# Loading w, k and r in runs of steps and turning them on VectorE in squares of 32, in a tuned attention-and-MLP kernel

One core of one Trainium2 chip. The metric is the device time of one execution in microseconds (us), the median of the runs of one kernel. All numbers from profiles are from one profiled execution of the kernel named.

## The reference

Attention by a recurrence with a decay, then a layer norm and a two-layer MLP with a residual. All in float32.

```python
batch, n_heads, seq, head_dim = (4, 8, 768, 48)

def _attn_ref(r, k, v, w, u):
    state = zeros((B, H, D, D)); y = zeros_like(r)
    for t in range(S):
        kt, vt, rt, wt = k[:, :, t], v[:, :, t], r[:, :, t], w[:, :, t]
        cur = einsum('bhd,bhe->bhde', u[None] * kt, vt)
        y[:, :, t] = einsum('bhd,bhde->bhe', rt, state + cur)
        state = wt[:, :, :, None] * state + einsum('bhd,bhe->bhde', kt, vt)
    return y

def _moe_ref(x, g_ln, w_ch1, w_ch2):            # x: (4, 768, 384)
    mu = mean(x); var = mean((x - mu) ** 2)
    xn = (x - mu) / sqrt(var + 1e-06) * g_ln
    return x + maximum(xn @ w_ch1, 0.0) @ w_ch2  # 384 -> 1536 -> 384
```

## The kernel before

The work is cut into eight **rounds** (four batches, two halves of 384 steps each). A round has two **units** of four heads, a unit two **pairs** of heads. Each round goes through six **levels**: in each, PE multiplies k by r for growing blocks of steps (`a_ps`), and VectorE multiplies r and k by the decay of the block (`grow`) and keeps the new part of the block matrix (`keep`). PE is TensorE, DVE VectorE, ACT ScalarE, POOL GpSimd; SP is the engine whose queue (SPq) issues 255 of the 260 transfers that the profile of before lists, PSUM the memory that PE's products are put in here (the tiles named `_ps`). The MLP of the round before is cut into small steps that are put between the levels, so that PE never runs dry. Each level has a list of **tasks** that is spread over its MLP steps: loads, turns, norms. In the timelines below each engine works through its instructions in program order: in the changed kernel POOL has the products for an own sum ready at 143.1 us, but DVE sums them at 162.23, behind eight squares that stand ahead of the sum, six of which wait for their loads.

The products need r, k and w with the head's dimension across partitions, the arrays have it along the row. So each tile is loaded with 128 steps across partitions, 192 bytes a row, and turned by PE. One **turn** below is one pair of one tensor of one unit: three matmuls and a copy (cuts are marked with `...`):

```python
def load(q, which="wkr", eng=SP):
    for nm in which:
        for c in range(TT):                       # TT = 3 tiles of 128 steps
            eng.dma_start(out=nat[nm][q % 2][:, c, :, 0:D], in_=steps(src_of(nm), q, c))

def turned(q, nm, pr):                            # one pair of one tensor of one unit
    ...
    ps = ps_t.tile([P, RN], F32, tag="t", ...)    # PSUM, two buffers
    for c in range(TT):
        PE.transpose(ps[:, ts(c, P)], nat[nm][q % 2][:, c, ts(pr, 2)]..., ident)
    ACT.copy(out=a[nm][:, ts(pr, RN)], in_=ps)

def own_products(q, eng):                         # POOL reads k and r as loaded
    rk = st[q]["ruk"] = p1.tile([P, TT, NH, D], F32, tag="rk", ...)   # p1: ONE buffer
    eng.tensor_tensor(out=rk, in0=nat["k"]..., in1=nat["r"]..., op=ALU.mult)
    ...
def own_sums(q):
    DVE.tensor_reduce(out=o, in_=st[q]["ruk"], axis=AX.X, op=ALU.add)
```

The tasks that matter, in the loop over rounds and levels:

```python
first = 3 if rnd == 2 else 1
if rnd > 1 and new and first <= lev < first + 3:
    m = lev - first                               # w, then k and r of one unit, then of the other
    tasks += each(turned, new[m - 1 : m], "kr", pairs) if m else each(turned, new, "w", pairs)
...
if lev == 3 and rnd > 1:
    ...
    if rnd > 2:
        moments(rnd - 1)
        tasks += each(norm, [rnd - 1])            # xn of the round before, on DVE
if lev == 4 and rnd > 2:
    tasks += each(turned_x, [rnd - 1], range(KC)) # PE turns xn for the MLP
    tasks += each(own_products, new[:1], [POOL])
...
if lev == NLEV - 1:                               # level 5
    ...
    if rnd > 2 and new:
        own_sums(new[0])
    if rnd == 2:
        tasks += each(own_products, new[:1], [POOL]) + each(own_sums, new[:1])
    ...
    tasks += each(own_products, new[1:], [POOL])  # needs the rk buffer back
    tasks += each(own_sums, new[1:]) + ...
```

So the turns for round `rnd + 1` stand in levels 1 to 3 of round `rnd`; only in round 2, for round 3, they stand in levels 3 to 5.

Of the kernel before, what the change touches and what calls it, by code (L numbers as in the profile page):

```python
# [9 lines left out]
F32 = mybir.dt.float32  # L10
# [42 lines left out]
def kernel(  # L53
# [13 lines left out]
    PE, ACT, DVE, POOL, SPO = (  # L67
        InOrder(tc, e) for e in (nc.tensor, nc.scalar, nc.vector, nc.gpsimd, nc.sync)
    )
    SP = nc.sync  # L70

    B, H, S, D = r.shape
    P = 128
    HP = 64
    C = 64
    NH = 4
    NP = NH // 2
    U = H // NH
    TT = 3
    RN = TT * P  # L80
# [3 lines left out]
    W = NK * P  # L84
# [6 lines left out]
    pairs = range(NP)  # L91
# [3 lines left out]
    p1 = ctx.enter_context(tc.tile_pool(name="p1", bufs=1))  # L95
    p2 = ctx.enter_context(tc.tile_pool(name="p2", bufs=2))
    p3 = ctx.enter_context(tc.tile_pool(name="p3", bufs=3))
    p4 = ctx.enter_context(tc.tile_pool(name="p4", bufs=4))
# [8 lines left out]
    units = [(b, f, g) for b, f in rounds for g in range(U)]  # L107
    NU = len(units)
# [24 lines left out]
    def load_rows(nm, q, eng):  # L133

        b, f, g = units[q]
        src = {"w": w, "k": k, "r": r}[nm]
        eng.dma_start(
            out=flat(nm, q)[:, 0 : NH * TT * D].rearrange("p (h x) -> p h x", h=NH),
            in_=src[b, ts(g, NH), ds(f * RN, RN)].rearrange("h (p c) d -> p h (c d)", c=TT),
        )  # L140

    def load_v(q, eng=SP):
        vn[q] = p4.tile([P, TT, NH, D], F32, tag="v", name=f"v{q}")
# [21 lines left out]
    for j in range(2):  # L165
        ACT.dma_start(
            out=sel[ds(HP * j, D), :, j], in_=u.rearrange("(r j) d -> j d r", j=2)[j]
# [23 lines left out]
    for lev in range(NLEV - 1):  # L191
        n = 1 << lev
        m = const.tile([P, C // n, n], I8, name=f"mask2_{lev}")
# [109 lines left out]

    st, carry = {}, {}

    def turned(q, nm, pr):
        a = st.setdefault(q, {})
        if pr == 0:
            if nm == "w":
                if q % U == 0:  # L310
                    st["w"] = p1.tile([P, U, W], F32, tag="w", name=f"wT{q // U}")
                a["w"] = st["w"][:, q % U]
            elif "rk" not in a:

                rk = a["rk"] = p4.tile([P, 2, W], F32, tag="rkT", name=f"rkT{q}")
                a["r"], a["k"] = rk[:, 0], rk[:, 1]
        ps = ps_t.tile([P, RN], F32, tag="t", name=f"{nm}_ps{q}_{pr}")
        if q < U:


            for c in range(TT):
                for j in (1, 0):
                    at = ((2 * pr + j) * TT + c) * D - HP * j
                    PE.transpose(
                        ps[0 : HP * (j + 1), ts(c, P)],
                        flat(nm, q)[:, ds(at, HP * (j + 1))], ident,
                    )
            (DVE.tensor_copy if q == 0 and pr else ACT.copy)(
                out=a[nm][:, ts(pr, RN)].rearrange("p (m c) -> p m c", c=TT),
                in_=ps.rearrange("p (c m) -> p m c", c=TT),  # L330
            )
            return
        for c in range(TT):
            PE.transpose(
                ps[:, ts(c, P)],
                nat[nm][q % 2][:, c, ts(pr, 2)].rearrange("p j d -> p (j d)"), ident,
            )
        ACT.copy(out=a[nm][:, ts(pr, RN)], in_=ps)
# [371 lines left out]
    def each(f, *ranges):  # L710
        calls = [()]
        for r_ in ranges:
            calls = [c + (x,) for c in calls for x in r_]
        return [lambda c=c: f(*c) for c in calls]
# [106 lines left out]
    for rnd in range(1, NR + 1):  # L821
        old, now, new = units_of(rnd - 1), units_of(rnd), units_of(rnd + 1)
        if rnd == 1:
            old = []
        for lev in range(NLEV):
            slot = (rnd - 1) * NLEV + lev
            if rnd == 2:

                for q in old if lev < 2 else []:
                    (states, outputs)[lev](q)  # L830
                if lev < 2:
                    mlp_step()
            elif old and lev < 2 * U:
                (states if lev < U else outputs)(old[lev % U])
                if lev >= U and now:
                    mlp_step()
            for q in now:
                if slot:
                    quads(q, lev)
            for which in ("rk",) if lev < NLEV - 1 else "kr":  # L840
                for q in now:
                    grow(q, lev, which)
            if now:
                if rnd == 1 and lev == 0:
                    totals(rnd, DVE)
                keep(rnd, lev)
            tasks = []
            if rnd == 1:
                if lev < 2:
                    tasks += each(load, new, "kr"[lev], [SPO])  # L850
                if lev == 2:
                    SPO.dma_start(
                        out=u_bc,
                        in_=bass.AP(
                            tensor=u.tensor, offset=u.offset, ap=[[0, P], [D, H], [1, D]]
                        ),
                    )
                    tasks += each(load_v, now, [SPO])
                if lev == 3:
                    tasks += each(load_vx, now, [SPO])  # L860
                if lev == 1:
                    tasks += each(product_sums, now)
                if lev in (4, 5):
                    own_term(now[lev - 4], POOL)
            if rnd == 2 and lev == 0:
                tasks += each(load_v, now) + each(load, new, "w")
            if rnd == 2 and lev == 2:
                for q in now:
                    take(DVE, q)
                    tasks += each(load, new[q % U :][:1], "kr")  # L870
            if rnd == 2 and lev in (3, 4):
                tasks += each(own_term, now[lev - 3 :][:1], [POOL])
            if rnd > 2 and lev < 2:
                tasks += each(load, new, ["w", "kr"][lev])
            first = 3 if rnd == 2 else 1
            if rnd > 1 and new and first <= lev < first + 3:
                m = lev - first
                tasks += each(turned, new[m - 1 : m], "kr", pairs) if m else each(
                    turned, new, "w", pairs
                )  # L880
            if rnd == 2:
                if lev == 0:
                    tasks += each(exchanged, old)
                if lev == 1:
                    tasks += [lambda: moments(1), lambda: norm(1)]
                if lev == 2:
                    tasks += each(turned_x, [1], range(KC))
            elif old and lev < U:
                tasks += each(exchanged, [old[lev]])
            if lev == 3 and rnd > 1:  # L890
                for q in now:
                    load_vx(q)
                for q in new:
                    load_v(q)
                if rnd > 2:
                    moments(rnd - 1)
                    tasks += each(norm, [rnd - 1])
            if lev == 4 and rnd > 2:
                tasks += each(turned_x, [rnd - 1], range(KC))
                tasks += each(own_products, new[:1], [POOL])  # L900
            if lev == NLEV - 1:

                if now:
                    mlp_step()
# [4 lines that stand above are left out]
                if rnd >= 2:  # L909
                    tasks += each(own_term, new[:1], [POOL])  # L910
                    tasks += each(own_products, new[1:], [POOL])
                    tasks += each(own_sums, new[1:]) + each(own_term, new[1:], [POOL])
                    if new:
                        tasks += each(totals, [rnd + 1], [POOL])
                if now:
                    tasks = mixed(
                        tasks,
                        each(ends, now, pairs) + each(finish, [2, 2, 4])
                    )
                if rnd == 1:  # L920
                    tasks = [join] * JOINS[lev] + tasks + each(totals, [rnd + 1], [POOL])
            if rnd == 1 and lev < NLEV - 1:

                n = (1, 2, 2, 1, 0, 0)[lev] * NP
                tasks += mixed([begin] * BEGINS[lev], [join] * JOINS[lev], ahead[:n])
                del ahead[:n]
            fill(UNTIL[slot], tasks)
            if lev == (2 if rnd == 2 else 4) and old:
                mlps.append(mlp(rnd - 1))
# [32 lines left out]
```

## Time and profile before

| kernel before | |
|---|---|
| time | 588.12 us, median of 3 runs (586.3 to 589.29) |
| span of the profiled run | 583.9 us |
| bytes moved | 36.52 MB |
| busy: PE, DVE, ACT, POOL | 98%, 47%, 33%, 16% |
| waits of PE from 117 us on | 1.6 us in all |

The page's chain that ended last (shares of the span by engine):

```profile
PE 91%; ACT 4%; DVE 2%; issue 1%; DMA 1%; ACTq 0%; DVEq 0%
```

### The profile page before, as it was taken

To read this page: it belongs to the slowest core of one execution; us is meant where nothing else is said; L and a number is where in the kernel's file an instruction comes from. 1 tells how busy PE (TensorE), PEld (TensorE's weight loads), DVE (VectorE), ACT (ScalarE), POOL (GpSimd) and SP (SyncE) were. 2 spreads that over 40 slices of the span, in tenths; PEclk is the share of its full clock that TensorE was granted. 3 is DMA by queue.
4 is the path that set the end of the run, shared out by engine and by line. 5 is a ranking of instruction groups with operands and counts; after the bars stand their busy time and mean duration, and the time that the engine had idled before them with its cause. 6 is when DMAs were issued, how large, how long until landed. Compare 5 with 4: busy or idle time off the path is not lost.

```text
span 583.9 us, 19053 instructions
## 1 busy us (share of the span) xinstructions
PE 572.2 (98%) x8558; PEld 384.1 (66%) x8558; DVE 273.6 (47%) x576; ACT 193.8 (33%) x423; POOL 90.6 (16%) x124
## 2 busy tenths in 40 slices
PE   9999989999999999999999999999999999999997
PEld 7876756666666766666766666666666666666554
DVE  4879898687273634343452543336254531130000
ACT  3577686313442234311432125312331015202200
POOL 6140011104440035000620007000320000000000
PEclk9899899999999999999999999999999999999999
DMA  9938684036315311340204302031000000000000
GB/s 230 203 102 178 175 239 117 16 78 137 64 22 102 72 36 21 68 92 15 57 8 89 65 29 43 2 64 28 15 2 2 16 28 2 2 15 27 0 15 27
DMA packets 114192, 36.52 MB, mean 63 GB/s; under 512 B 104768, under 2 KB 111040, under 8 KB 114112
## 3 DMA queue, kind: packets, MB, share of 16 engines
q1 hardware_dynamic: 112240, 34.72, 26.5%
q8 instruction: 67, 1.10, 0.8%
q10 hardware_dynamic: 1872, 0.59, 0.4%
q14 instruction: 13, 0.11, 0.1%
HBM read 28.51 MB, written 4.72 MB: 57 GB/s over the span
## 4 chain that ended last, share of the span: by engine, by line
PE 91%; ACT 4%; DVE 2%; issue 1%; DMA 1%; ACTq 0%; DVEq 0%
PE o_ps L49 32%; PE h_ps L49 30%; PE a_ps L49 11%; PE y L49 4%; PE kv L49 2%; PE k_ps L49 2%; PE r_ps L49 2%; PE w_ps L49 2%; PE kn_ps L49 2%; PE xT_ps L49 1%; ACT rest L49 1%; PE own_ps L49 1%; PE idle L49 1%; ACT rkT L49 1%; ACT w_sb L49 1%
## 5 line engine op out<-in xcount | busy, mean ns | idle before, releaser
L49 PE MATMUL o_ps<-w_sb,h 128*128 128x384 f32 x576 | 199.0, 490 | 0.9 <-ACT h L49 0.9
L49 PE MATMUL h_ps<-xT,w_sb 128*128 128x384 f32 x576 | 198.7, 493 | 0.0
L49 PEld LDWEIGHTS h_ps<-xT,w_sb 128*128 128x128 f32 x576 | 105.7, 191 | 63.1 <-issue 0.9
L49 PEld LDWEIGHTS o_ps<-w_sb,h 128*128 128x128 f32 x576 | 104.4, 190 | 62.0 <-ACT h L49 1.8
L49 DVE TENSOR_TENSOR rkT<-rkT,tot 128x768 f32<-128x768 f32 (+1 forms) x96 | 76.7, 841 | 38.9 <-issue 26.0
L49 ACT ACTIVATE h<-h_ps 128x384 f32<-128x384 f32 x96 | 46.8, 488 | 144.7 <-PE h_ps L49 144.6
L49 PEld LDWEIGHTS a_ps<-rkT 48*64 48x64 f32 x4608 | 73.2, 136 | 20.8 <-issue 13.4
L49 PE MATMUL a_ps<-rkT 48*64 48x32 f32 x4608 | 78.4, 221 | 0.1
L49 DVE TENSOR_TENSOR o<-o_ps,x 128x384 f32<-128x384 f32 x24 | 13.4, 557 | 121.9 <-PE o_ps L49 121.8
L49 POOL TENSOR_TENSOR vo<-v,own 128x576 f32<-128x576 f32 x16 | 19.2, 1203 | 288.7 <-DVE own L49 251.9
L49 DVE SCALAR_TENSOR_TENSOR s<-s,decay,kv 128x48 f32<-128x48 f32 x160 | 29.3, 259 | 33.9 <-PE kv L49 33.9
L49 DVE TENSOR_TENSOR x<-y,vo 128x288 f32<-128x288 f32 x32 | 13.2, 453 | 53.8 <-PE y L49 53.7
L49 DVE COPY_PREDICATED A<-mask,a_ps 128x768 f32<-128x768 int8 x32 | 38.3, 1197 | 0.0
L49 ACT COPY rkT<-k_ps 128x384 f32<-128x384 f32 x31 | 13.9, 478 | 57.3 <-PE k_ps L49 57.1
L49 ACT ACTIVATE xT<-xT_ps,g_sb 128x384 f32<-128x384 f32 x24 | 13.6, 579 | 54.0 <-PE xT_ps L49 54.0
L49 ACT COPY rkT<-r_ps 128x384 f32<-128x384 f32 x31 | 14.2, 478 | 24.2 <-PE r_ps L49 24.1
L49 DVE TENSOR_SCALAR w_sb<-w_sb 128x384 f32<-128x384 f32 (+1 forms) x48 | 19.5, 406 | 0.8
L49 ACT ACTIVATE rstd<-mv,eps 128x3 f32<-128x3 f32 x8 | 2.4, 296 | 49.2 <-DVE mv L49 49.1
L49 DVE TENSOR_REDUCE own<-rk 128x12 f32<-128x576 f32 x12 | 9.0, 750 | 20.7 <-POOL rk L49 20.6
L49 ACT COPY wT<-w_ps 128x384 f32<-128x384 f32 x31 | 14.0, 478 | 14.1 <-PE w_ps L49 14.1
L49 PE MATMUL r_ps<-ident,nat_r 128*128 128x128 f32 x108 | 16.2, 279 | 2.2 <-ACT rkT L49 2.1
L49 DVE TENSOR_TENSOR rkT<-rkT,wT 128x768 f32<-128x768 f32 x16 | 17.5, 1131 | 0.9 <-PE a_ps L49 0.8
(76 smaller groups left out, 517.9 us busy)
## 6 DMA issues: line engine op xcount, KB each, us to landing
raw<-in_moe_w_ch_dram SPq DMA_DIRECT2D x24, 384.0 KB, 4.3
v<-in_v_dram SPq DMA_DIRECT2D x48, 96.0 KB, 3.3
out_dram<-o SPq DMA_DIRECT2D x24, 192.0 KB, 1.9
nat_w<-in_w_dram SPq DMA_DIRECT2D x42, 96.0 KB, 2.9
nat_r<-in_r_dram SPq DMA_DIRECT2D x42, 96.0 KB, 2.8
nat_k<-in_k_dram SPq DMA_DIRECT2D x42, 96.0 KB, 3.1
vx<-v SPq DMA_DIRECT2D x28, 72.0 KB, 2.3
nat_r<-in_r_dram ACTq DMA_DIRECT2D x2, 288.0 KB, 4.9
```

Source lines behind the costliest of these rows:

```text
L49: return lambda *args, **kw: self.tc.keep_in_program_order(f(*args, **kw))
```

## The change

The intent: take 180 transposes off PE, which is the bound, and give the turning to VectorE, which is half idle. The new kernel has VectorE turn squares of 32x32 (60 instructions STREAM_TRANSPOSE of 128x384). Its data come in another form: each partition gets a run of 12 consecutive steps (560 floats, 2240 bytes), 32 partitions to a transfer, four transfers to a tile. One instruction then turns twelve squares of each block of 32 partitions and writes with a step of 12 floats, 48 bytes; one such instruction is called a **square** below, and it takes the place of one turn. ("Run" with a number means an experiment, "runs" the data.) The runs are loaded one level before they are turned, into the four buffers that the MLP weights went through earlier. k and r are still loaded in the old form too, for POOL.

```diff
+    SQ = 32
+    NS = RN // SQ                     # 12
+    ROW = (NS - 1) * D + SQ           # 560
+    def stage(q, nm, pr, eng=SP):
+        ...
+        t = p4.tile([P, WC, 2], F32, tag="raw", ...)          # 4 buffers
+        for j in range(2):
+            first = src.offset + ((b * H + g * NH + 2 * pr + j) * S + f * RN) * D
+            for e in range(HP // SQ):
+                ...
+                eng.dma_start(
+                    out=t[ds(HP * j + SQ * e, SQ), 0:n],
+                    in_=bass.AP(tensor=src.tensor, offset=first + SQ * e,
+                                ap=[[NS * D, SQ], [1, n]]))
+    def squares(q, nm, pr):
+        DVE.transpose(
+            out=a[nm][:, ts(pr, RN)].rearrange("p (t s) -> p s t", s=NS),
+            in_=staged.pop((q, nm, pr)).rearrange("p (s d) -> p s d", s=NS)[..., 0:SQ])
 ...
             if rnd == 2 and lev == 0:
-                tasks += each(load_v, now) + each(load, new, "w")
+                tasks += each(load_v, now)
-            if rnd > 2 and lev < 2:
-                tasks += each(load, new, ["w", "kr"][lev])
+            if rnd > 2 and lev == 1:
+                tasks += each(load, new, ["kr"])
             first = 3 if rnd == 2 else 1
-            if rnd > 1 and new and first <= lev < first + 3:
+            if rnd > 1 and new and first - 1 <= lev < first + 3:
                 m = lev - first
-                tasks += each(turned, new[m - 1 : m], "kr", pairs) if m else each(
-                    turned, new, "w", pairs
-                )
+                turns = [(new, "w"), (new[:1], "kr"), (new[1:], "kr")]
+                if m >= 0:
+                    tasks += each(squares, *turns[m], pairs)
+                if m < 2:
+                    tasks += each(stage, *turns[m + 1], pairs)
```

More of the change, by code (lines that the diff above doesn't have):

```diff
@@ L140, in load_rows @@
         )
+    SQ = 32
+    NS = RN // SQ
+    ROW = (NS - 1) * D + SQ
+    staged = {}
+    def stage(q, nm, pr, eng=SP):
+        b, f, g = units[q]
+        src = {"w": w, "k": k, "r": r}[nm]
+        t = p4.tile([P, WC, 2], F32, tag="raw", name=f"{nm}_runs{q}_{pr}")
+        t = staged[q, nm, pr] = t.rearrange("p n two -> p (n two)")[:, 0 : NS * D]
+        for j in range(2):
+            first = src.offset + ((b * H + g * NH + 2 * pr + j) * S + f * RN) * D
+            for e in range(HP // SQ):
+                n = ROW
+                if (q, pr, j, e) == (NU - 1, NP - 1, 1, 1):
+                    n = NS * D - SQ
+                    POOL.memset(t[P - SQ :, n:], 0.0)
+                eng.dma_start(
+                    out=t[ds(HP * j + SQ * e, SQ), 0:n],
+                    in_=bass.AP(
+                        tensor=src.tensor, offset=first + SQ * e, ap=[[NS * D, SQ], [1, n]]
+                    ),
+                )
     def load_v(q, eng=SP):
@@ L304, with turned_to @@
     st, carry = {}, {}
-    def turned(q, nm, pr):
-        a = st.setdefault(q, {})
-        if pr == 0:
-            if nm == "w":
-                if q % U == 0:
-                    st["w"] = p1.tile([P, U, W], F32, tag="w", name=f"wT{q // U}")
-                a["w"] = st["w"][:, q % U]
-            elif "rk" not in a:
-                rk = a["rk"] = p4.tile([P, 2, W], F32, tag="rkT", name=f"rkT{q}")
-                a["r"], a["k"] = rk[:, 0], rk[:, 1]
+    def turned_to(q, nm):
+        a = st.setdefault(q, {})
+        if nm == "w":
+            if q % U == 0:
+                st["w"] = p1.tile([P, U, W], F32, tag="w", name=f"wT{q // U}")
+            a["w"] = st["w"][:, q % U]
+        elif "rk" not in a:
+            rk = a["rk"] = p4.tile([P, 2, W], F32, tag="rkT", name=f"rkT{q}")
+            a["r"], a["k"] = rk[:, 0], rk[:, 1]
+        return a
+    def squares(q, nm, pr):
+        a = st[q] if pr else turned_to(q, nm)
+        DVE.transpose(
+            out=a[nm][:, ts(pr, RN)].rearrange("p (t s) -> p s t", s=NS),
+            in_=staged.pop((q, nm, pr)).rearrange("p (s d) -> p s d", s=NS)[..., 0:SQ],
+        )
+    def turned(q, nm, pr):
+        a = st[q] if pr else turned_to(q, nm)
         ps = ps_t.tile([P, RN], F32, tag="t", name=f"{nm}_ps{q}_{pr}")
```

## The prediction

> **What bounds the kernel now.** I read the page's busy shares first, then the slices, the waits of PE after the start, the timeline of one level, and last the groups by form.
>
> The page of the kernel before, its busy line (engine, busy us, share of the span, instructions) and the slices of PE, DVE and the granted clock:
>
> ```profile
> PE 572.2 (98%) x8558; PEld 384.1 (66%) x8558; DVE 273.6 (47%) x576; ACT 193.8 (33%) x423; POOL 90.6 (16%) x124
> ...
> PE   9999989999999999999999999999999999999997
> ...
> DVE  4879898687273634343452543336254531130000
> ...
> PEclk9899899999999999999999999999999999999999
> ```
>
> PE is busy everywhere and DVE half the time. "Busy" is not proof that PE is the bound, so I asked what PE waited for from 117 us on (waiter, what it waited for, us in total, times, longest):
>
> ```profile
> PE k_ps L49 <- ACT rkT L49: 0.6, 1, 0.6
> PE r_ps L49 <- ACT rkT L49: 0.5, 2, 0.3
> PE kn_ps L49 <- ACT kn L49: 0.3, 1, 0.3
> PE kn_ps L49 <- ACT rkT L49: 0.2, 1, 0.2
> ```
>
> That is 1.6 us of waiting in 467 us. From round 2 on the kernel is PE's instruction stream, end to end: work taken out of it comes off the time, and work put on another engine is free until it makes PE wait. The chain that ended last agrees: 91% of it is PE.
>
> **What one removed turn really costs PE.** Three matmuls turn one pair of heads (one head pair, one tensor, 384 steps). The group line says 280 to 292 ns each, which would make 180 of them 51 us. I do not take that number. The timeline of PE between 382.7 and 390 us (start, length, what):
>
> ```profile
> 382.74 0.87 PE L49 MATMUL k_ps<-ident,nat_k 128*128 128x128 f32 x6
> 383.45 2.10 PE L49 MATMUL o_ps<-w_sb,h 128*128 128x384 f32 x6
> 385.38 0.49 PE L49 MATMUL r_ps<-ident,nat_r 128*128 128x128 f32 x3
> 385.71 2.10 PE L49 MATMUL o_ps<-w_sb,h 128*128 128x384 f32 x6
> 387.65 0.49 PE L49 MATMUL r_ps<-ident,nat_r 128*128 128x128 f32 x3
> 387.98 2.10 PE L49 MATMUL o_ps<-w_sb,h 128*128 128x384 f32 x6
> ```
>
> Read the starts, not the lengths: 385.38 to 385.71 and 387.65 to 387.98 are 0.33 us for three transposes, 0.11 each; six in a row take 0.71 (382.74 to 383.45) here and 0.66 elsewhere. The following six MLP matmuls take 1.94 us from start to start whether or not a transpose stands before them, so nothing more is lost at the change-over.
>
> [...] the new transposes write with a step of 48 bytes, and no row of before shows what that costs DVE. I keep it as a doubt on the size.
>
> **The change, part by part.** Units are rounds times two; rounds 3 to 7 are 5 rounds, so 5 x 2 units x 3 tensors x 2 pairs = 60 turns.
>
> 1. Removed from PE: 60 x 3 = 180 transposes with their weight loads. They stand at about 140 us and later: 132 of the 312 after 178 us (48 for r, 48 for k, 36 for w), the other 48 before. 60 x 0.33 = 19.8 us by the clean spacing, 60 x 0.355 = 21.3 us by the looser one. All of it is on the path.
>
> 2. Removed from ACT: 60 copies from PSUM at 478 ns, 28.7 us. ACT is 33% busy and makes PE wait 1.6 us at most; worth nothing, or up to 1 us in round 2, where near 155 us four turns and four transposes of kn fight for the two PSUM buffers.
>
> 3. Added to DVE: 60 transposes of 128x384. The groups by form, rows of that shape (after the bar: busy us, mean ns; then idle before and its releaser):
>
> ```profile
> L49 DVE TENSOR_TENSOR o<-o_ps,x 128x384 f32<-128x384 f32 x24 | 13.4, 557 | 121.9 <-PE o_ps L49 121.8
> L49 DVE TENSOR_TENSOR rkT<-rkT,tot 128x384 f32<-128x384 f32 x32 | 16.3, 555 | 8.8 <-issue 6.1 <-PE a_ps L49 2.0
> ```
>
> Both take 0.556 us for 384 elements a partition, from PSUM or SBUF alike; the 768-element rows take 984, so the rate is 1.1 ns an element and the rest fixed. I take 0.557 for a transpose of the same size. 60 x 0.557 = 33.4 us, so DVE goes from 274 to about 307 us of a span near 564, 54%. If the 48-byte steps double it, 67 us and 60%. Four stand in each of three levels of a round, so 2.2 us (or 4.5) are added to a level of about 10.5 us.
>
> 4. Moved on the queue: 30 loads of w in rows of 192 bytes go (10 units x 3); 60 x 4 = 240 transfers of 32 partitions x 2240 bytes come. k and r are still loaded the old way too, because the POOL products read them. Bytes grow by about 60 x 128 x 2240 = 17.2 MB less 2.9 MB, so 36.5 becomes about 51 MB in the span, 90 GB/s against up to 239 GB/s seen in a slice. The issue is the dearer side: a weight load (128 rows of 3 KB) holds the queue 0.34 us in its median, so 16 issues are 5.5 us in each of three levels per round, which fits a level but is not small.
>
> Sum: 588.1 - 19.8 to 21.3, with up to 1 us more and perhaps 1 us of new waits: 567 to 568 us.
>
> **The rivals.**
>
> Rival A, DVE becomes a wait for PE. The timeline of DVE in level 2 (start, length, what, idle before):
>
> ```profile
> 314.42 1.83 DVE L49 TENSOR_TENSOR rkT<-rkT,tot 128x768 f32<-128x768 f32 x2 [2.22 <-issue]
> 316.16 0.97 DVE L49 COPY_PREDICATED A<-mask,a_ps 128x768 f32<-128x768 int8 x1
> 322.30 0.56 DVE L49 TENSOR_TENSOR o<-o_ps,x 128x384 f32<-128x384 f32 x1 [5.17 <-PE o_ps L49]
> ```
>
> The squares stand right behind the second row in DVE's order. It ends at 317.1, DVE next works at 322.3, and four squares end at 319.4. In level 3 it is tighter: keep, moments and norm follow one another from 259 to 265.5, the sum for o stands at 267 and the next growth at 267.9, which the PE needs only at 277.3. Four squares push these by about 0.7 us (3 us if doubled), against some 7 us of slack. So against it: the slack; for it: it repeats five times. It would cost 0 to 5 us.
>
> Rival B, DVE stalls on a late load. DVE is in order, and a square whose run hasn't landed blocks all behind it. Four buffers serve all runs, so the loads of one level can only start as the squares of that level free them, and must land before the next level's. From the squares' end (about 305 us in level 1) to the next squares (317) are 12 us; the 16 issues (5.5) and a landing like the 2.8 to 3.1 us of the old loads make 8.5. It holds, with 2 to 4 us to spare, less in level 3. If the queue is slower than I think (0.49 us per issue, as the loads of nat_r show, or a run stuck behind a store that waits), each late level could cost PE 1 to 3 us, 15 levels: 5 to 15 us, so 573 to 583.
>
> Rival C, the busy time was real, that is PE gains the 51 us[...]: 537 us. The spacings speak against it plainly, and the granted clock is at 1.00 in all stages after 117 us.
>
> **Range and chances.** The gain of 20 us is as good as counted; the doubt is all in what of it A and B give back, and in the 3 us by which the runs of before differ (586.3 to 589.3). 2% is 11.8 us, so under 576.4 is "faster"; it takes a give-back of 8 us to miss it, which is only B at its worse end. I set 567.5 us, 8 in 10 between 563.5 and 574.0, faster 0.89, same 0.09, slower 0.02.
>
> **What would show each step.** The PE lines of r_ps, k_ps and w_ps fall from 324 to 144 matmuls, and a round (67.7 us from 309.8 to 377.5 by the y matmuls) shrinks to about 63.7. The transposes on DVE show 0.5 to 0.6 us each[...]. PE's waits after 117 us stay under 3 us. If instead PE waits for DVE rkT or x, A is right; if DVE's transposes are preceded by idle time ended by a DMA, and PE waits behind them, B is. If PE is without waits and the gain still isn't near 20 us, my cost of a turn is wrong.

(One slip in it: "132 of the 312 after 178 us". The 132 is right, 48 + 48 + 36; the 312 stands for nothing that I can find. That DVE is in order was seen afterwards: in the changed kernel the last square of level 5 waited 1.57 us for its run, until 161.51 us, and the own sum behind it, whose products had been there since 143.1, began at 162.23. What a square takes was an estimate from the two rows shown, and the doubling by the 48-byte step no more than a what-if.)

## More of the kernel before

The timeline of DVE at the end of round 2 (start, length, what, and in brackets the idle time before it and what ended that) will be needed later:

```profile
150.74 2.14 DVE L49 TENSOR_TENSOR rkT<-rkT,tot 128x384 f32<-128x384 f32 x4 [6.08 <-issue]
152.80 0.75 DVE L49 TENSOR_REDUCE own<-rk 128x12 f32<-128x576 f32 x1
157.68 0.75 DVE L49 TENSOR_REDUCE own<-rk 128x12 f32<-128x576 f32 x1 [4.13 <-POOL rk L49]
162.58 0.32 DVE L49 COPY s<-kv 128x48 f32<-128x48 f32 x2 [4.14 <-PE kv L49]
```

The growth of level 5, then the two own sums of round 3, then the first state of the round. The second own sum waits 4.1 us for POOL: there is one `rk` buffer, so POOL can begin the products of the second unit only when DVE has summed the first's (sum from 152.80 to 153.55 us, those products from 154.73). But DVE has been idle before all of this and waits for PE at the end of it. That is slack. Both own sums stand in level 5 of the later rounds too, with the same wait of 4.1 us for POOL; but it is in round 2 alone that turns stand in level 5 as well, ahead of them.

## The result

| | median us | lowest to highest | ratio to before, 95% interval |
|---|---|---|---|
| before | 588.54 (4 runs) | 586.3 to 589.29 | |
| after | 581.83 (4 runs) | 580.95 to 582.37 | 0.9891 (0.986 to 0.9921) |
| predicted | 567.5 | 563.5 to 574.0 | |

A ratio here and below is the mean time of one kernel's fast runs over that of the other's of the same rounds, so not quite the ratio of the medians. The change is worth 6.7 us where 20.6 were predicted, and counts as "same". Some 14 us are missing. The outputs are right.

The page of the changed kernel: busy line, granted clock, chain.

```profile
PE 560.5 (97%) x8378; PEld 370.7 (64%) x8378; DVE 317.3 (55%) x636; ACT 168.6 (29%) x363; POOL 94.5 (16%) x127
...
PEclk9889799999997989999999999999999999999999
...
PE 81%; DVE 6%; ACT 4%; SPq 3%; DMA 3%; issue 2%; POOL 0%; ACTq 0%; DVEq 0%
```

The 180 matmuls are gone, and the bytes are as predicted: 50.78 MB in place of 36.52. But PE's part of the chain fell from 91 to 81%: DVE, the queue that issues transfers (SPq) and the transfers now stand in it. And the clock row has a 7 and an 8 in slices 13 and 15 (counted from 1; 174 to 188 us and 203 to 217 us), where before there were only nines.

**Where the time went.** I read the starts of the growth products of each level from PE's timeline and cut the span at two of them:

| stretch | before | after | difference |
|---|---|---|---|
| start to level 1 of round 2 | 119.3 | 121.3 | +1.9 |
| from there to level 2 of round 4 | 126.2 | 129.4 | +3.1 |
| from there to the end | 338.3 | 328.6 | -9.7 |

The first row is not the change's: the stretch has spells of half clock (granted clock 0.50) before too, and their sum differs from profile to profile: 10.2 us (before), 13.7 (after), none in run 3's, 17.1 in run 6's. Half of the difference of the two, since 0.50 was granted, is 1.7 us. The last row is the predicted gain at work. In one round of it the three levels with turns fell from 14.43, 12.48 and 8.80 us to 13.11, 11.21 and 7.53: 1.27 to 1.32 us for four turns, 0.32 to 0.33 us each. On PE's timeline the products and the MLP follow each other with nothing between them (the same level of the kernel before, from 313.39 us on, had the twelve matmuls of its four turns there, in three groups):

```profile
314.96 1.60 PE L49 MATMUL a_ps<-rkT 48*64 48x32 f32 x96
316.49 6.07 PE L49 MATMUL o_ps<-w_sb,h 128*128 128x384 f32 x18
```

The loss is in the middle row: rounds 2 and 3 and the first of round 4's three levels with turns. 28 of the 60 turns left PE there, and it still took longer. What PE waited for from 117 us on (in the kernel before these waits came to 1.6 us; here to 9.4, of which 1.0 is a wait at 118.4 us that before has too, at 116.5, just outside this window), and what DVE's squares waited for:

```profile
PE a_ps L49 <- DVE s L49: 3.0, 1, 3.0
PE xT_ps L49 <- DVE xn L49: 2.1, 1, 2.1
...
DVE rkT L49 <- DMA r_runs<-in_r_dram: 4.3, 4, 1.6
DVE rkT L49 <- DMA k_runs<-in_k_dram: 1.6, 2, 1.2
```

Two single waits of PE stand out. Both can be followed back.

**The first stall.** The queue's timeline from 143 us on, where round 2 is in its level 4 (start, length of a group of issues, what):

```profile
143.48 3.58 SPq L163 DMA_DIRECT2D k_runs<-in_k_dram  x8
147.17 4.42 SPq L163 DMA_DIRECT2D r_runs<-in_r_dram  x8
151.68 3.62 SPq L163 DMA_DIRECT2D k_runs<-in_k_dram  x8
155.40 4.57 SPq L163 DMA_DIRECT2D r_runs<-in_r_dram  x8
160.08 8.51 SPq L163 DMA_DIRECT2D w_runs<-in_w_dram  x16
```

Eight issues take 3.6 to 4.6 us, 0.45 to 0.57 each on average (most start 0.46 us apart, one in some groups takes over 0.9), so the sixteen of a level take 8.2 us. For round 3 those of w were issued long before they were needed (95.6 to 104.4 us). Those of k and r stand among the tasks of levels 3 and 4 of round 2, which last 7.6 and 7.5 us on PE; in a steady round levels 1 and 2, where they stand, have 13.1 and 11.2 us. And they don't start sooner: the queue stood idle from 139.9 us until 143.48, when the first square of w (142.60 us, 0.85 long) had freed one of the four buffers. From there it runs back to back and the data comes behind. DVE's timeline at the same place:

```profile
153.12 0.85 DVE L49 STREAM_TRANSPOSE rkT<-r_runs 128x384 f32<-128x384 f32 x1 [0.82 <-DMA r_runs<-in_r_dram]
153.82 1.92 DVE L49 TENSOR_TENSOR rkT<-rkT,tot 128x384 f32<-128x384 f32 x4
...
159.08 0.87 DVE L49 STREAM_TRANSPOSE rkT<-r_runs 128x384 f32<-128x384 f32 x1 [1.33 <-DMA r_runs<-in_r_dram]
161.51 0.86 DVE L49 STREAM_TRANSPOSE rkT<-r_runs 128x384 f32<-128x384 f32 x1 [1.57 <-DMA r_runs<-in_r_dram]
162.23 0.70 DVE L49 TENSOR_REDUCE own<-rk 128x12 f32<-128x576 f32 x1
167.03 0.75 DVE L49 TENSOR_REDUCE own<-rk 128x12 f32<-128x576 f32 x1 [4.11 <-POOL rk L49]
```

Compare with DVE's timeline of before, shown above. The growth of level 5 starts 3.1 us later, because DVE is still at the squares of level 4. Then come four squares with waits for the runs between them, and the first own sum starts at 162.23 instead of 152.80. POOL's turn-around of 4.1 us is the same as ever, but now nothing hides it: the second own sum is at 167.03, the states and the growth of level 0 follow, and PE gets its operands at 173.78. The stall and the next one in PE's timeline:

```profile
173.78 2.79 PE L49 MATMUL a_ps<-rkT 48*64 48x32 f32 x96 [2.98 <-DVE s L49]
...
206.64 1.73 PE L49 MATMUL xT_ps<-ident,xn 128*128 128x128 f32 x6 [2.10 <-DVE xn L49]
```

**The second stall.** In level 3 of round 3 four squares stand ahead of the norm in DVE's order (202.7 to 205.9 us; xn from 206.1). The level is only 5.6 us long, and PE asks for xn at 204.5.

**The clock after the stalls.** The same kernel in stretches (stretch, its length, busy us with counts for PE, its weight loads, DVE, ACT and POOL, then granted clock, DMA share, GB/s):

```profile
172.00:174.00 2.00, 0.22 (x9) 0.26 (x12) 2.00 (x6) 0.00 (x0) 1.74 (x4) 0.88 0.94 161
174.00:176.00 2.00, 2.00 (x84) 2.00 (x84) 2.00 (x11) 0.62 (x2) 1.59 (x2) 0.50 1.11 181
```

Right after each wait PE works at half clock: the clock records of the profile have 0.50 from 173.5 to 180.3 us, 6.8 us after the first, and from 207.6 to 211.1, 3.4 us after the second. The records of the two profiles, before's and this one's, hold 0.50 and 1.00 and nothing else, and every spell of 0.50 in them lasts 3.4 or 6.8 us (but for the last record of each, 2.5 and 2.3 us, which starts 0.4 us before the end of the span and 0.4 after it). The prediction had left this out.

So the theory after reading: **late runs (issues, not bytes) cause the first stall, the order of norm and squares the second, and each stall costs its length and a spell of half clock on top.** Rivals: the squares are simply too long for DVE (0.84 us against 0.557 assumed); the bytes compete; the clock falls by chance and has nothing to do with the stalls. Not tested is the number of buffers by itself: from the queue's idle time, 139.9 to 143.48 us, my estimate is that more of them would let the same issues start up to 3.6 us sooner.

### The profile page after: what moved, and what is told of

Same layout as the page of the kernel before. It is cut to its first block, busy times and chain, and to the rows that moved or that the text cites. A ratio compares the mean times of both kernels' runs of the same rounds, so it can differ in the third digit from the quotient of the medians.

```text
span 579.2 us, 19006 instructions
## 1 busy us (share of the span) xinstructions
PE 560.5 (97%) x8378; PEld 370.7 (64%) x8378; DVE 317.3 (55%) x636; ACT 168.6 (29%) x363; POOL 94.5 (16%) x127
## 2 busy tenths in 40 slices
DMA packets 109875, 50.78 MB, mean 88 GB/s; under 512 B 92768, under 2 KB 99040, under 8 KB 109792
## 4 chain that ended last, share of the span: by engine, by line
PE 81%; DVE 6%; ACT 4%; SPq 3%; DMA 3%; issue 2%; POOL 0%; ACTq 0%; DVEq 0%
PE o_ps L49 30%; PE h_ps L49 27%; PE a_ps L49 10%; PE y L49 4%; DVE rkT L49 3%; PE kv L49 2%; SPq L163 2%; DMA v<-in_v_dram 2%; PE kn_ps L49 2%; PE xT_ps L49 1%; ACT rest L49 1%; PE own_ps L49 1%; SPq L173 1%; PE idle L49 1%; PE r_ps L49 1%
## 5 line engine op out<-in xcount | busy, mean ns | idle before, releaser
L49 PEld LDWEIGHTS o_ps<-w_sb,h 128*128 128x128 f32 x576 | 107.3, 193 | 67.9 <-issue 3.0
L49 DVE TENSOR_TENSOR rkT<-rkT,tot 128x768 f32<-128x768 f32 (+1 forms) x96 | 79.3, 867 | 28.3 <-issue 15.5
L49 ACT ACTIVATE xT<-xT_ps,g_sb 128x384 f32<-128x384 f32 x24 | 13.7, 580 | 55.3 <-PE xT_ps L49 55.3
L49 DVE TENSOR_REDUCE own<-rk 128x12 f32<-128x576 f32 x12 | 8.9, 746 | 20.6 <-POOL rk L49 20.6
L49 DVE STREAM_TRANSPOSE rkT<-r_runs 128x384 f32<-128x384 f32 x20 | 15.7, 837 | 4.3 <-DMA r_runs<-in_r_dram 4.3
L49 PEld LDWEIGHTS kv<-v,kn 64*64 64x64 f32 x768 | 12.7, 134 | 8.2 <-issue 6.2
L49 PEld LDWEIGHTS y<-v,A 64*64 64x64 f32 x384 | 13.3, 137 | 7.1 <-issue 4.4
L49 DVE TENSOR_TENSOR rkT<-rkT,wT 128x768 f32<-128x768 f32 x16 | 17.1, 1107 | 0.9 <-PE a_ps L49 0.8
L49 DVE STREAM_TRANSPOSE rkT<-k_runs 128x384 f32<-128x384 f32 x20 | 15.8, 849 | 1.7 <-DMA k_runs<-in_k_dram 1.6
```

Source lines behind the costliest of these rows:

```text
L49: return lambda *args, **kw: self.tc.keep_in_program_order(f(*args, **kw))
```

## The experiments

Each was run against the kernel before on the same chip, in four batches (1 to 4, 5 to 8, 9 to 11, 12). "Stretch" is the time in the profile from the start of level 1 of round 2 to the end of the span; it leaves out the start, whose spells of half clock differ from profile to profile. Before has 464.6, the changed kernel 458.0. A profile is one execution, so differences of the stretch under about 1 us aren't read. The edits are shortened: lines are joined or left out. The times that were expected were missed in runs 1 to 3, 5 to 7 and 9, by 0.1 to 4.7 us, and run 8's lay between its two answers; the readings rest on the waits and stretches of the profiles.

**1. Idle matmuls in both stalls** (the same data, a correct result), to hold the clock up.

```diff
+            if rnd == 3 and lev == 1:
+                warm(24, "t")
             for q in now: quads(q, lev)
 ...
+            if lev == 4 and rnd == 3:
+                tasks.append(lambda: warm(15, "t"))
             if lev == 4 and rnd > 2: tasks += each(turned_x, ...)
```

> The changed kernel with eight idle matmuls of 384 columns ahead of the level-1 growth products of round 3 (where PE waited 3.0 us for the states) and five ahead of the turns of x in round 3 (where it waited 2.1 us). No wait of the engines is touched. Theory (short PE waits, each followed by a stretch at half clock): the clock of 0.50 between 173 and 180 us and between 207 and 211 us goes, each is worth half its length, 3.4 and 1.7 us; the time falls from 581.8 to 576.5 to 579 us. Rival (the half clock has other causes, or the clock is not what costs): the dips stay and the time is 581 to 584 us.

Measured: 579.08 us (575.97 to 581.83), ratio 0.9874 (0.9793 to 0.9956), stretch 457.4. Both spells of half clock are gone. But I had counted an idle matmul at half of what it takes; the first block ran 5.46 us where the hole was 3:

```profile
168.88 5.46 PE L49 MATMUL idle<-nought 128*128 128x384 f32 x16
```

It shows that the spells follow the idle time; the time it leaves inconclusive. Run 11 repeats it with fewer.

**2. The norm ahead of the squares** in level 3 (correct).

```diff
-                    tasks += each(norm, [rnd - 1])
+                    tasks[:0] = each(norm, [rnd - 1])
```

> The normalisation of level 3 stands ahead of the four squares of that level in DVE's order; nothing else. Theory: the wait of PE for xn (2.1 us at 205 us) and the half clock behind it (1.7 us) go, and the later rounds win some 0.3 us each; 577 to 579 us. Rival (DVE is only late there because of a load, or the wait moves to the next growth): 581 to 583 us.

Measured: 573.7 us (572.23 to 578.86), ratio 0.979 (0.9719 to 0.9861), stretch 453.5. The wait for xn and the spell after it are gone, the first stall of 3.0 us and its 6.8 us of half clock stay. So the second stall is the order alone, and is worth 4.5 us in the stretch: 2.1 of wait, 1.7 (half of 3.4) of clock, and the rest in later rounds, where level 4, in which PE turns xn, had grown by some 0.35 us each (10.42 before, 10.77 after, 10.41 here).

**3. Four tiles loaded once**, all squares read those (wrong result): squares without late loads.

```diff
+        if len(once) == 4:
+            staged[q, nm, pr] = once[...]
+            return
         t = p4.tile([P, WC, 2], F32, tag="raw", ...)
```

> Wrong result on purpose: the four runs of w of round 3 are loaded once, and all 60 squares read them; 224 of the 240 transfers go, every square keeps its size and place. Theory of late loads (a transfer holds the queue 0.45 to 0.57 us, so 16 take more than a level of round 2): the waits of DVE for r_runs and k_runs (5.9 us) go, PE's wait of 3.0 us before 173.8 us goes with them, and so does its half clock; 574 to 577 us. Rival (DVE's own time makes the stalls): the waits on loads go but PE's waits stay; 580 to 582 us.

Measured: 569.31 us (566.78 to 569.62), ratio 0.969 (0.9632 to 0.9747), stretch 446.95. No square waits for a load and the first stall is gone, with the squares as long as ever. The wait for xn stays at 2.0 us. So the length of the squares alone doesn't make the first stall. This one takes away issues and bytes alike; run 5 parts them. In its profile there is no half clock up to the last 0.3 us, so a wait of 2 us isn't always followed by a spell.

**4. Squares that write contiguously** (wrong): the cost of the 48-byte step.

```diff
-            out=a[nm][:, ts(pr, RN)].rearrange("p (t s) -> p s t", s=NS),
+            out=a[nm][:, ts(pr, RN)].rearrange("p (s t) -> p s t", s=NS),
```

> Wrong result on purpose: the squares write 32 steps next to each other instead of 48 bytes apart; same count, same loads, same reads. If the step of 48 bytes is what makes a square 0.85 us: 0.50 to 0.56 us each, 18 us less work on DVE, PE's wait for xn shrinks from 2.1 to under 1 us, and the time is 576 to 580 us. If the transpose itself is slow: 0.80 to 0.85 us each and 581 to 583 us.

Measured: 577.0 us (576.11 to 580.89), ratio 0.9843 (0.9779 to 0.9908), stretch 455.0. The groups by form, first of the changed kernel, then of this one (after the bar: busy us, mean ns; then the idle time before and its releaser):

```profile
L49 DVE STREAM_TRANSPOSE rkT<-r_runs 128x384 f32<-128x384 f32 x20 | 15.7, 837 | 4.3 <-DMA r_runs<-in_r_dram 4.3
```

```profile
L49 DVE STREAM_TRANSPOSE rkT<-r_runs 128x384 f32<-128x384 f32 x20 | 10.4, 547 | 6.9 <-DMA r_runs<-in_r_dram 6.9
```

A square costs 0.55 us contiguous, what the prediction took, and 0.84 with the step; 0.29 us times 60 is 17.5 us of DVE. Given this time back, DVE only waits longer for the runs (6.9 us instead of 4.3), and the first stall stays at 3.0 us. The rival "too long squares" falls for the first stall; for the second the length counts (1.2 us instead of 2.1). Both spells of half clock stay, 6.8 and 3.4 us, the second now behind a wait of only 1.2 us.

**5. One transfer to a tile**, 128 partitions, the same bytes, a quarter of the issues (wrong, since this pattern reads other rows).

```diff
-        for j in range(2): for e in range(HP // SQ): eng.dma_start(32 partitions)
+        eng.dma_start(out=t[:, 0:ROW], in_=bass.AP(..., ap=[[S * D // P, P], [1, ROW]]))
```

> Wrong result on purpose: each of the 60 tiles of runs comes in one transfer of 128 partitions x 2240 bytes instead of four of 32; the same bytes, the same buffers and squares, 60 issues on the queue instead of 240. Theory (the queue's time per issue, some 0.45 to 0.57 us, makes the loads of round 2 late): as good as the kernel that loads once, 569 to 572 us, and no wait of DVE for runs over 0.5 us. Rival (the bytes or the landing make them late): 578 to 582 us, DVE waits for r_runs as before.

Measured: 573.93 us (571.48 to 576.12), ratio 0.9778 (0.9739 to 0.9818), stretch 449.3. Waits of PE and of the squares:

```profile
PE xT_ps L49 <- DVE xn L49: 2.0, 1, 2.0
...
PE a_ps L49 <- DVE s L49: 0.4, 1, 0.4
...
DVE rkT L49 <- DMA k_runs<-in_k_dram: 0.9, 2, 0.7
DVE rkT L49 <- DMA r_runs<-in_r_dram: 0.2, 1, 0.2
```

The waits for runs fall from 5.9 to 1.1 us and the first stall from 3.0 to 0.4, with every byte still moved. It was the **number of issues**. The second stall, and 3.4 us of half clock after it, are untouched. The same four buffers were used and the first of these issues stood at 143.32 us (143.48 in the changed kernel), so with 4 issues in place of 16 to a level this start could be afforded. An issue for 128 partitions took no longer than one for 32: median of the records 0.34 and 0.42 us, and the groups of two for k and r from 143 to 178 us took 0.83 to 1.02 us.

**6. Both pairs of a unit in one transfer** (correct): 32 partitions by 2 runs, half the issues; three double buffers instead of four single ones, so one less on the way of the weights.

```diff
-        t = p4.tile([P, WC, 2], F32, tag="raw", ...)
+        t = p3.tile([P, NP, NS * D], F32, tag="raw", ...)
 ...
-                    ap=[[NS * D, SQ], [1, n]]
+                    ap=[[NS * D, SQ], [2 * S * D, NP], [1, ROW]]
```

> A right kernel: both pairs of heads of a tensor in one transfer (32 partitions x 2 x 2240 bytes), so 121 transfers instead of 240, three buffers of double size instead of four. Theory of issues: 16 issues of a level become 8, some 4 us, and fit; PE's wait of 3.0 us and its half clock go, 570 to 575 us, the rest being PE's wait for xn. Rival (landing or bytes): 578 to 582 us.

Measured: 575.82 us (574.45 to 576.9), ratio 0.981 (0.9779 to 0.9842), stretch 448.45. No square waits for a run, the first stall is gone, the second (2.1 us and its half clock) stays. The stretch gains 9.5 us on the changed kernel; the start loses 5, level 1 of round 2 beginning at 126.4 us instead of 121.3; 1.7 of the 5 is half clock (17.1 us of it there, 13.7 in the changed kernel). Run 12 undoes the changes to the weights' buffers.

**7. Round 3 turned the old way**, rounds 4 to 7 by squares (correct).

```diff
+            if rnd == 2 and first <= lev < first + 3:   # as in the kernel before
+                m = lev - first
+                tasks += each(turned, new[m - 1 : m], "kr", pairs) if m else each(turned, new, "w", pairs)
-            if rnd > 1 and new and first - 1 <= lev < first + 3:
+            if rnd > 2 and new and first - 1 <= lev < first + 3:
```

> Round 3 is loaded and turned as in the kernel before, on PE; rounds 4 to 7 by VectorE. 4 us of the PE's saving are given up. Theory (all of round 3's turns sit in round 2, where the queue and DVE are full): the stall of 3.0 us at 171 us, its 3.4 us of half clock and some 2 us of smaller waits go; net 577 to 580 us, slightly under the changed kernel. Rival (every round loses alike): 584 to 586 us.

Measured: 575.34 us (574.59 to 576.41), ratio 0.9805 (0.9776 to 0.9833), stretch 452.1. It gives up 12 turns, 4.0 us of the saving (12 x 0.33), and is still ahead of the changed kernel (0.9805 against 0.9891): the squares for round 3 cost more than they saved. The first stall is gone; the wait for xn stays at 2.1 us, this time without half clock after it.

**8. Round 3's loads and squares one level sooner** (correct).

```diff
-            first = 3 if rnd == 2 else 1
+            first = 2 if rnd == 2 else 1
```

> Round 3's runs are loaded and turned one level sooner in round 2 (squares in levels 2, 3, 4 instead of 3, 4, 5), so that level 5 with its sums of own terms is free of them. Issue count unchanged. If what hurts is that the late squares hold up the sums of level 5 and through them POOL and the states: the wait of 3.0 us goes, 574 to 578 us. If the loads are simply too many for round 2: a wait of that size shows one level sooner and the time stays at 580 to 583 us.

Measured: 578.08 us (576.62 to 579.18), ratio 0.9846 (0.9809 to 0.9883), stretch 455.4. The stall moved:

```profile
PE kn_ps L49 <- DVE rkT L49: 3.6, 1, 3.6
PE h_ps L49 <- DVE o L49: 2.5, 1, 2.5
```

The wait for xn is there too, and the squares still wait 6.6 us for runs. Starting earlier didn't help: the issues are as many as before (8.2 us for the sixteen of a level in the changed kernel, whose levels 2 and 3 of round 2, where those of k and r now stand, last 9.1 and 7.6 us), and both waits of PE are for DVE. The wait of 3.6 us was followed by 3.4 us of half clock, those of 2.5 and 2.1 us by none.

**9. Runs 6 and 2 together** (correct, 5 rounds). The edit is theirs.

> A right kernel: two pairs in one transfer and the normalisation ahead of the squares, the two repairs together. Theory: both stalls of PE after 120 us and the half clock behind them are gone, PE waits under 3 us in all after 120 us, and the gain is what the transposes cost on PE, some 20 us: 566 to 570 us, as the prediction had it, with a few us of spread from half clock in the first 90 us. Rival (the repairs don't add up, something else binds): 572 to 575 us.

Measured: 572.02 us (568.7 to 574.93), ratio 0.9745 (0.9705 to 0.9785), stretch 443.7. That is 20.9 us less than before, the whole of the predicted saving; PE waits 2.5 us after 117 us and has no half clock after 100. What keeps it from 567 is the slow start of run 6.

**10. The changed kernel again**, 5 rounds, on the same chip.

> The changed kernel unaltered, on the same chip and in the same rounds as the repaired ones. 579 to 583 us if the first measurement was typical; the half clock at 173 and 207 us shows again if the stalls cause it, while that of the first 90 us may differ.

Measured: 579.33 us (577.17 to 583.53), ratio 0.9882 (0.9841 to 0.9922), stretch 457.9. Both stalls, 3.0 and 2.1 us, and both spells of half clock, 6.8 and 3.4 us, are there again. They are not chance.

**11. Fewer idle matmuls** in the stalls (correct): `warm(12)` and `warm(6)` in the places of run 1.

> As the first run with idle matmuls, but half as many (an idle one took 0.68 us, twice what I had counted, and the block of 5.5 us overran the stall of 3): 2.7 us of them before the growth products of round 3, 1.4 us before its turns of x. Theory (half clock is a cost of its own, on top of the waits): no half clock at 173 and 207 us, and 4 to 5 us less from the level at 121 us to the end than the changed kernel beside it (458.0 us before). Rival: under 1.5 us less.

Measured: 575.04 us (573.07 to 578.12), ratio 0.98 (0.9757 to 0.9843), stretch 453.05. No half clock follows the two places, and the stretch is 4.85 us shorter than in run 10. The delays are still there: the idle matmuls only stand in them, and the squares wait for runs for 7.7 us (6.5 in run 10). So the clock is a cost of its own of about 5 us. Half of 6.8 + 3.4 us is 5.1.

**12. Both repairs with the start as it was** (correct): pairs in one transfer, norm first, but four buffers for the weights as in the changed kernel; the third double buffer lies in the space of w's old tile, free from round 2 on, and round 3's w and first k are loaded in program order at level 0 of round 2.

```diff
+    raw_all = const.tile([P, 4 * 768], F32, name="raw_all")
+    bufs = [raw_all[:, 0:DB], raw_all[:, DB : 2 * DB], nat_w.rearrange(...)[:, 0:DB]]
 ...
+                        ap=[[NS * D, SQ], [2 * S * D, NP], [1, ROW]]
 ...
-                tasks += each(load_v, now)
+                tasks += each(load_v, now) + each(stage, new, "w", [0], [SPO])
+                tasks += each(stage, new[:1], "k", [0], [SPO])
 ...
-                    tasks += each(norm, [rnd - 1])
+                    tasks[:0] = each(norm, [rnd - 1])
```

> A right kernel, the two repairs as before, but the weights' raw words keep four buffers and their rest four, as in the kernel before; the third double buffer of the runs lies in the space of the w that is loaded the old way for rounds 0 to 2. Theory (the pairs cost about 4 us in the first 120 us only because there were three raw buffers): the level that begins at 119 to 121 us before and in the changed kernel begins there again and not at 126 us, the rest takes 443 to 445 us as in the run before this, together 565 to 569 us. Rival (the slow start was chance, from half clock in the first 90 us): no gain over 572 us in the median.

Measured: 566.82 us (564.28 to 568.75, 6 runs) against 586.57 (583.12 to 589.43, 11 runs), ratio 0.9659 (0.9622 to 0.9696), stretch 443.5. It beats both kernels. Its chain, and all it has of waits of PE after 117 us:

```profile
PE 93%; ACT 3%; DVE 2%; DMA 1%; issue 1%; ACTq 0%; DVEq 0%
...
PE y L49 <- issue: 1.3, 1, 1.3
PE kn_ps L49 <- ACT kn L49: 0.6, 2, 0.3
PE xT_ps L49 <- ACT xT L49: 0.3, 1, 0.3
```

## Why the prediction was wrong

**Right: PE is the bound, and a turn costs its slot.** 0.32 to 0.33 us per turn in the steady rounds, and 20.9 and 21.1 us over the stretch in runs 9 and 12, where nothing gives them back (though DVE was busy 314.5 us in run 12 against 273.6 before). The predicted sum was 19.8 to 21.3. Rival C is out.

**Right: the ACT copies are worth next to nothing (PE's waits for them, 1.3 us in all before, are gone in run 12), the bytes are about 51 MB** (50.78 measured), DVE goes to 55%. The bytes as such hurt nothing (run 5: 50.75 MB moved, the first stall 0.4 us).

**Wrong: "It holds, with 2 to 4 us to spare".** This is the step that failed: rival B, late loads. It was named, with the very sign that then stood in the trace and with a time of 573 to 583 us, and its chance was set far too low. Three things were wrong in it:

- The issue. I took 0.34 us from the weight loads, although the loads of nat_r showed 0.49 and I quoted it. Measured 0.45 to 0.57: 8.2 us for a level, not 5.5.
- The place. I worked out the slack from levels of a steady round, where the issues have over 10 us each. In round 2 those of k and r have 7.5 to 7.6, and behind the squares stand the two own sums with POOL's turn-around between them, which the change laid bare. Steady rounds do hold, as I said: all six waits of squares for runs in the profile (5.9 us) are of the squares of levels 4 and 5 of round 2.
- The size of a square: 0.557 us assumed, 0.84 measured. The doubt was named; it adds to the second stall (run 4), not to the first.

**Rival A came too, small.** PE waits for xn for 2.1 us in round 3 and some 0.35 us in each later round; I had given it 0 to 5 us. The 7 us of slack that I counted on were those of the next growth; I hadn't asked when PE needs xn, and round 3's level 3 has only 5.6 us in all.

**Missing: the clock.** No term of the sum said that a wait of 2 to 3 us on PE may cost as much again in half clock. About 5 us (run 11).

**The balance**, in the stretch, changed kernel against run 12 (458.0 - 443.5 = 14.5 us): PE's waits inside it are 8.4 against 0.9 (the first one after 117 us lies before it in both), so 7.5 us; half of 10.2 us of half clock, 5.1; from level 2 of round 4 on, 328.6 against 327.6, 1.0. That leaves 0.9 us unplaced. The first stall was shown to come from the issues (runs 3, 5, 6), the second from the order (run 2), the clock from the stalls (runs 1, 11).

Why was a wait of about 2 us followed by half clock in some profiles (the changed kernel, runs 5, 6 and 10) and not in others (runs 3, 7 and 8)? No run tests it, but the clock records that came with the profiles speak to it. In each profile all spells begin on one grid of 3.41 us (in the changed kernel's the five starts before the last lie 5, 6, 33 and 10 times 3.41 us apart). In the first four the wait lies almost wholly between two lines of that grid (in the changed kernel 204.5 to 206.6, between 204.2 and 207.6); in the other three a line cuts it (in run 7 200.6 to 202.7, the line at 201.6). Counted over all fourteen profiles from 117 to 540 us, the nine intervals of that grid at full clock with under 1.4 us of busy PE (0.7 and 1.2 us in the changed kernel; two in run 10 as well, one each in runs 2, 4, 5, 6 and 8) were all followed by half clock; of those with 1.8 us or more only one was (run 4's, with 2.1). So in these profiles the length of a wait alone didn't decide; this is a pattern in the records and not an experiment.

## What to carry to other kernels

A change that moves work off the bound engine must hold in the tightest place it touches, not the typical one: look for the shortest level that has the new work and for the chain that stands behind it on the same engine. Count issues of a queue by the dearest duration in the trace and set them against the length of the level, for the number of transfers, not the bytes, may be what is late: here the same bytes in a quarter of the issues took the first stall from 3.0 to 0.4 us (run 5). And a stall of PE can cost as much again: where half clock followed one of 1.2 to 3.6 us here, it lasted 3.4 or 6.8 us, and the two of the changed kernel, 5.1 us of waits, were followed by 10.2 us of it, whose end was worth 4.85 us (run 11).
